# Converting w1 and w2 in the attention, and one operand's sum moved ahead of its split, in an attention and two-MoE kernel

## The chip, the cores and the metric

The kernel runs on one core of a Trainium2 chip. The core has a matrix engine (TensorE, PE in the profile; its weight loads are listed as PEld), a vector engine (VectorE, DVE), a scalar engine (ScalarE, ACT), a general engine (GpSimd, POOL) and a queue engine that here issues the transfers (SyncE, SP). Each takes its instructions in order and waits on semaphores for the others. The metric is the device time of one execution in microseconds (us); lower is better.

## The reference

Three stages follow one another. The inputs are float32, except the weights, which come as float64.

```python
# 1: attention with a local band and a few global columns, 4 x 8 heads of 768 x 64
scores = scale * q @ k.T + bias          # bias: -slope[h] * distance
a = softmax(where(keep, scores, -1e9))   # keep: column < 8, or 0 <= row - column < 96
x = a @ v                                # 3072 tokens x 512
# 2: first MoE layer, w_in 512 x 2048, w_out 2048 x 512
h = x @ w_in
x = (h * clip(h + 3, 0, 6) / 6) @ w_out
# 3: second MoE layer, w1 and w2 512 x 1024, w3 1024 x 1024, w_out 1024 x 512
out = ((x @ w1) * (x @ w2)) @ w3 @ w_out
```

## The kernel before

**Numbers.** Matmuls take a value as two parts, a high half rounded by ScalarE and a low half (the value less the high half), and a product is three matmuls: high by high, low by high, high by low. The low halves are made on VectorE or GpSimd. A weight comes as float64, 512 KB for 128 x 512 values. Its conversion to float32 is one ScalarE step (line 158, tile `cva`) and three VectorE steps on the raw bits (lines 171, 173 and 175, tile `cvt`).

**Weight jobs.** All weights go through one list of jobs, `wjobs`. A job is loaded by SyncE into a tile `st` (three buffers), converted, and handed to what it is for. `w_steps` does this in rounds of four ticks, and the code that writes the order calls `tick` in between: 4 ticks per step of the attention while the first weights are awaited, 2 after that, so one job for two steps; in the MoE stage a tick for every 0.5 or 1.2 us of TensorE's work. At a round a job waits for its load in ScalarE's queue (line 158), and in the next rounds its VectorE steps are written. A job whose source is float32 skips these four steps and gets to its use after as many rounds.

**The attention** runs 96 steps, two to a pair of score matmuls (line 419). A step's scores go through a maximum on VectorE (429), an exponential on ScalarE (438), a normalisation on GpSimd (446), a transpose and the product with v. A filler puts matmuls of the first MoE layer (half of its columns, `gen_a`) between. Sixteen pieces of w_in and w_out for the other half are converted here too and kept in DRAM (`wb`, line 591: a store from `cvt`).

**The rest of the first MoE layer** follows from 440 us on, in eight passes of 384 tokens, each `first` (gates: line 513 on ScalarE, 514 on VectorE, halves 497 and 500) and `second`, whose results are added up on VectorE (line 832, `part`), which frees the accumulators. Beside it, w3 times the last w_out is made (`gen_w34`), and w1 and w2 are prepared in sixteen quarters (`wt_job`): three VectorE sums (lines 687 to 689), then high halves on ScalarE (184) and low halves on GpSimd (185) of the quarter and of the sums. The quarters of the first two groups stay in place; the others go to DRAM and back.

**The second MoE layer** takes two token blocks at a time as a 2 x 2 problem with seven products in place of eight (`gen_ab`), for two groups of columns (`gg`), and then multiplies by the w3 and w_out product (`gen_out`). The seven token operands of the next pair are made meanwhile by `x_prep`: seven pieces, each a VectorE sum or nothing, then `put`, which makes the high half on ScalarE (783) and the low half on GpSimd (784). One piece is called after each of the products 6, 7, 5, 2, 4 and 3 of the second group, the seventh after the first two output blocks. Six of the eight pairs are followed by another one and so have pieces; before the first pair, `weave` puts the seven pieces between the last matmuls of `second`.

`s[0]` holds first a21 + a22, which is operand 5 and the start of `s[1]`, and then a12 - s[1], operand 3. The fourth piece was

```python
def s1():
    put(5, s[0])                                                  # ScalarE and GpSimd read s[0]
    nc.vector.tensor_tensor(s[0], a12, s[1], ALU.subtract)        # line 797 writes it
```

After each product VectorE adds it to the sums (line 901) and, for finished ones, multiplies both halves (896); the result is split into `g4` to `g7` for `gen_out`.

Of the kernel before, what the change touches and what calls it, by code (L numbers as in the profile page):

```python
# [8 lines left out]
F32 = mybir.dt.float32  # L9
# [8 lines left out]
P = 128  # L18
# [56 lines left out]
def kernel(ctx: ExitStack, tc: tile.TileContext, q, k, v, n_global, n_local,  # L75
# [12 lines left out]
    NF2 = DF2 // P  # L88
# [3 lines left out]
    FB = NF - FA  # L92
# [12 lines left out]
    dr = ctx.enter_context(tc.tile_pool(name="dr", bufs=1, space=DRAM))  # L105
# [5 lines left out]
    w34 = dr.tile([NF2, 2, P, DM], F32, name="w34")  # L111
    wt = dr.tile([NF2, 4, P, 512], F32, name="wt")
    part2 = dr.tile([NT, DM], F32, name="part2")
    wb = dr.tile([2 * FB, P, 512], F32, name="wb")

    WA = [wap.tile([P, 512], F32R, name=f"wa{i}") for i in range(4 * FA)]

# [11 lines left out]
    def queue(src, then, key=None):  # L129
        wjobs.append((src, then, key))  # L130
        queued.add(key)
# [51 lines left out]
    def w_split(t, hi, lo, key):  # L183
        nc.scalar.activation(hi, t, AF.Copy)  # L184
        (nc.vector if key[0] in first_weights else nc.gpsimd).tensor_tensor(lo, t, hi.bitcast(F32), ALU.subtract)  # L185
# [404 lines left out]
    def keep(n):  # L590
        return lambda t, st: nc.sync.dma_start(wb[n], t)

    for n, (w, part) in enumerate([(w_in, kchunk)] * FB + [(w_out, rows)] * FB):
        queue(part(w, FA + n % FB), keep(n), ("wb", n))

    slot = FA * 24 * TA / per

    def nticks(s):
        return 1 if s < 4 else 4 if awaited("wi", "wo") else 2

    for s in range(NS + 3):
# [24 lines left out]
        n = nticks(s)  # L626
# [44 lines left out]
        fill.run(GAPS[0] / 4)  # L671
        tick()

    NG = NF2 // 2

    def wt_index(g, w, c):
        return (2 * g + w) * 2 + c  # L680

    def wt_job(n):
        def then(t, st):
            bl = t.rearrange("p (a c) -> p a c", c=P)
            tt = st.bitcast(F32)[:, 512:]
            tl = tt.rearrange("p (a c) -> p a c", c=P)
            nc.vector.tensor_tensor(tl[:, 0:2], bl[:, 1:4:2], bl[:, 0:2], ALU.subtract)
            nc.vector.tensor_tensor(tl[:, 2], bl[:, 3], tl[:, 0], ALU.subtract)
            nc.vector.tensor_tensor(tl[:, 3], bl[:, 2], tl[:, 2], ALU.subtract)
            to = WA[4 * n:4 * n + 4] if n < 8 else WA[24:28]  # L690
            for i, x in enumerate((t, tt)):
                w_split(x, to[i], to[2 + i], ("wt", n))

            def store():
                for i in range(4):
                    nc.sync.dma_start(wt[n - 8, i], to[i].bitcast(F32))
            if n >= 8:
                wstore.append(store)
        return then
# [6 lines left out]

    def wt_jobs(gs):
        for g in gs:
            for w, x in enumerate((w1, w2)):
                for c in range(2):  # L710
                    n = wt_index(g, w, c)
                    src = x.rearrange("(s c p) f -> c p s f", s=2, p=P)[c][:, :, 2 * g * P:2 * (g + 1) * P]
                    queue(src, wt_job(n), ("wt", n))

    quarters = [(w, c) for w in range(2) for c in range(2)]

    def gen_w34():

        ng = DF2 // 512
        for f in range(NF2):  # L720
            queue(rows(w_o2, f), O2[f], ("o2", f))
        wt_jobs([2])
        for f in range(NF2):
            for g in range(ng):
                queue(rows(w3, f)[:, g * 512:(g + 1) * 512], lambda t, st: got.append(t))
        wt_jobs([3])

        def trans(f):
# [12 lines left out]
        for f in range(NF2):  # L741
# [10 lines left out]
            for z in range(2):  # L752
                nc.sync.dma_start(w34[f, z], o[z].bitcast(F32))
        wt_jobs(range(NG // 2))

    def step(gen, gap=None):
# [20 lines left out]
    def x_prep(k, tmp):  # L777

        a11, a12, a21, a22 = (RA[i][:, 2 * c:2 * c + 2] for i in range(2) for c in range(2))
        s = [tmp() for _ in range(3)]  # L780

        def put(n, x):
            nc.scalar.activation(X[n][:, 0:2], x, AF.Copy)  # L783
            nc.gpsimd.tensor_tensor(X[n][:, 2:4], x, X[n][:, 0:2].bitcast(F32), ALU.subtract)  # L784

        def first_():
            nc.vector.tensor_tensor(s[0], a21, a22, ALU.add)  # L787
            nc.vector.tensor_tensor(s[1], s[0], a11, ALU.subtract)
            put(1, a11)

        def s3():
            nc.vector.tensor_tensor(s[2], a11, a21, ALU.subtract)  # L792
            put(7, s[2])

        def s1():
            put(5, s[0])
            nc.vector.tensor_tensor(s[0], a12, s[1], ALU.subtract)  # L797

        return [first_, lambda: put(6, s[1]), s3, s1, lambda: put(2, a12), lambda: put(4, a22),
                lambda: put(3, s[0])]  # L800

    def weave(gen, pieces, start, gap):

# [8 lines left out]
    for t in reversed(range(NTA)):  # L812
# [22 lines left out]
        if t == 0:  # L835
            fill.drain(pump)
            pump_all()
            flush()
            half.close()
            xo = fast.enter_context(tc.tile_pool(name="xo", bufs=1, side="right", reuse_waits="tile"))  # L840
            for n in range(5):
                X[1 + n] = xo.tile([P, CC, NA], F32R, name=f"x{n}")
            X[6], X[7] = xT[0]

            def st_tmp():
                t = cvp.tile([P, 1024], U32, tag="st", name="stmp", bufs=3)
                return t.bitcast(F32)[:, :2 * NA].rearrange("p (a n) -> p a n", a=2)

            pieces = x_prep(NTA // 2 - 1, st_tmp)
            gen = weave(gen, pieces, 600.0, 1800.0)  # L850
# [139 lines left out]
    for n, (p, j) in enumerate(order):  # L990
        nxt = order[n + 1][1] if n + 1 < len(order) else j
        pieces = x_prep(nxt, z_tmp) if nxt != j else []
        for gen in (gen_ab(p, j, nxt, pieces), gen_out(p, j, pieces)):
            for cost in gen:
                pass
        while pieces:
            pieces.pop(0)()
# [221 lines left out]
```

## Time and profile before

| | |
|---|---|
| median of three runs | 1223.22 us (1220.52 to 1224.03) |
| the profiled execution | 1222.52 us, its span 1220.7 us |
| TensorE busy | 1156.7 us, 95% |
| VectorE, ScalarE, GpSimd busy | 56%, 44%, 35% |
| mean granted clock of TensorE | 0.979 |
| HBM read, written | 112.72 MB, 51.38 MB |

Times inside the trace count from the first instruction. A wait is put down to the instruction that ended it; "idle before" in brackets is the time in which an engine stood before an instruction. A busy TensorE is not TensorE at its peak, since matmuls overlap: what it loses is read from the distance of the starts.

### The profile page before, as it was taken

Reading aid. Unit: us, or ns where it says so; the run is one execution under the profiler, and the core shown is the slowest. Engines: PE = TensorE matmul, PEld = TensorE weight load, DVE = VectorE, ACT = ScalarE, POOL = GpSimd, SP = SyncE. Lnnn points to the kernel's source line nnn. Section 1 sums busy time; section 2 is a strip of 40 time slices with the busy share of each in tenths; the row PEclk is TensorE's granted clock in tenths of the full one; section 3 lists DMA queues with packets and bytes.
Section 4 is the critical chain, followed back from the end, with each engine's and each line's share of the span. In section 5 each row is a group of like instructions: output and inputs, shape, how many; then the busy total and the mean of one; then the engine's idle time right before and its main releaser. Section 6 shows DMA issues by size and latency. Waiting matters only on the chain. (4 is left out here: it accounts for less than half of the span.)

```text
span 1220.7 us, 19580 instructions
## 1 busy us (share of the span) xinstructions
PE 1156.7 (95%) x7040; PEld 1070.3 (88%) x7040; DVE 679.3 (56%) x1495; ACT 535.4 (44%) x1282; POOL 430.3 (35%) x370
## 2 busy tenths in 40 slices
PE   6699999999999999998999998889999999999996
PEld 4488998999999999998899998889899899898895
DVE  4887766544444424368544374855374463565653
ACT  4787767666666645344324143441323311221310
POOL 2133334242333422256302044682443410533510
PEclk9699999999999999999999999999999999999998
DMA  7675867534253023456553556506203156134022
GB/s 167 186 224 140 227 166 219 174 78 130 56 145 78 6 71 121 173 183 231 190 183 94 189 190 224 174 18 222 86 19 104 46 186 218 52 105 155 14 90 90
DMA packets 185578, 165.50 MB, mean 136 GB/s; under 512 B 110720, under 2 KB 150656, under 8 KB 185472
## 3 DMA queue, kind: packets, MB, share of 16 engines
q1 hardware_dynamic: 185184, 164.15, 43.8%
q8 instruction: 58, 0.95, 0.3%
q14 instruction: 48, 0.39, 0.1%
q10 hardware_dynamic: 288, 0.00, 0.0%
HBM read 112.72 MB, written 51.38 MB: 134 GB/s over the span
## 5 line engine op out<-in xcount | busy, mean ns | idle before, releaser
L66 PE MATMUL b<-x,wa 128*128 128x384 f32 x960 | 173.4, 340 | 0.7 <-DVE part L832 0.7
L66 PEld LDWEIGHTS b<-x,wa 128*128 128x128 f32 x960 | 169.7, 188 | 1.7 <-issue 1.0
L446 POOL TENSOR_TENSOR e<-e,su 128x512 f32<-128x512 f32 (+1 forms) x96 | 93.0, 969 | 206.9 <-DVE su L445 169.4
L901 DVE TENSOR_TENSOR u<-b,u 128x768 f32<-128x768 f32 x112 | 105.2, 951 | 99.8 <-PE b L66 86.8
L514 DVE SCALAR_TENSOR_TENSOR t<-t,h 128x384 f32<-128x384 f32 x128 | 70.6, 551 | 125.7 <-ACT t L513 125.5
L438 ACT ACTIVATE e<-e,mx 128x256 f32<-128x256 f32 (+1 forms) x192 | 93.0, 492 | 15.7 <-DVE mx L429 15.3
L513 ACT ACTIVATE t<-h,c 128x384 f32<-128x384 f32 x128 | 73.8, 576 | 45.8 <-PE h L66 45.3
L158 ACT ACTIVATE cva<-st 128x512 f32<-128x512 f32 x72 | 48.1, 667 | 68.9 <-DMA st<-in_moe_w_dram 45.0
L429 DVE CUSTOM_DVE_ANT_0 e<-s,base 128x256 f32<-128x256 f32 (+1 forms) x192 | 69.1, 397 | 2.3 <-PE s L419 1.8
L175 DVE SCALAR_TENSOR_TENSOR cvt<-cva,cvt 128x512 uint32<-128x512 uint32 x72 | 67.3, 935 | 1.4
L66 PE MATMUL h<-xt0h,wa 128*128 128x384 f32 x256 | 67.9, 341 | 0.0
L66 PE MATMUL h<-xt1h,wa 128*128 128x384 f32 x256 | 67.2, 339 | 0.0
L472 PE MATMUL pv<-p,rv 128*64 128x128 f32 x704 | 53.8, 291 | 13.9 <-ACT p L461 13.9
L454 PE MATMUL pt<-ident,e 128*128 128x128 f32 x352 | 59.1, 290 | 7.3 <-DVE kl L360 4.6
L461 ACT ACTIVATE p<-pt 128x512 f32<-128x512 f32 (+1 forms) x96 | 55.0, 573 | 24.8 <-PE pt L454 24.6
L472 PEld LDWEIGHTS pv<-p,rv 128*64 128x64 f32 x704 | 38.9, 141 | 28.2 <-ACT p L461 16.7
L500 POOL TENSOR_TENSOR g0l<-t,g0h 128x384 fp32r<-128x384 f32 x16 | 18.0, 1123 | 127.9 <-ACT g0h L497 127.9
L173 DVE SCALAR_TENSOR_TENSOR cvt<-st,cvt 128x512 uint32<-128x512 uint32 x72 | 62.2, 864 | 1.1
L896 DVE TENSOR_TENSOR u<-u 128x384 f32<-128x384 f32 x64 | 60.3, 943 | 1.6
L185 POOL TENSOR_TENSOR wa<-cvt,wa 128x512 fp32r<-128x512 f32 x24 | 34.5, 1440 | 64.5 <-ACT wa L184 56.0
L454 PEld LDWEIGHTS pt<-ident,e 128*128 128x128 f32 x352 | 42.8, 148 | 15.2 <-issue 12.3
L500 POOL TENSOR_TENSOR g3l<-u,g3h 128x384 fp32r<-128x384 f32 x8 | 8.1, 1018 | 135.1 <-ACT g3h L497 135.1
(435 smaller groups left out, 3121.4 us busy)
## 6 DMA issues: line engine op xcount, KB each, us to landing
st<-in_moe_w_dram SPq DMA_DIRECT2D x32, 512.0 KB, 5.5
st<-in_moe_w_out_dram SPq DMA_DIRECT2D x24, 512.0 KB, 4.2
st<-in_moe_w_in_dram SPq DMA_DIRECT2D x16, 512.0 KB, 4.4
wt<-wa SPq DMA_DIRECT2D x32, 256.0 KB, 3.8
wa<-wt SPq DMA_DIRECT2D x32, 256.0 KB, 5.3
rk<-in_k_dram SPq DMA_DIRECT2D x64, 96.0 KB, 3.8
rq<-in_q_dram SPq DMA_DIRECT2D x64, 96.0 KB, 3.0
rv<-in_v_dram SPq DMA_DIRECT2D x64, 96.0 KB, 2.9
```

The lines of the kernel that those rows point to most:

```text
L66: nc.tensor.matmul(out, a, b, start=(first and i == 0 and j == 0), stop=(last and i == n - 1 and j == 2))
L173: nc.vector.scalar_tensor_tensor(tu, low, 29, tu, ALU.logical_shift_right, ALU.bitwise_or)
L175: nc.vector.scalar_tensor_tensor(tu, au, 0x80000000, tu, ALU.bitwise_and, ALU.bitwise_or)
L429: nc.vector.tensor_tensor_reduce(e[:, j, :W], d["sc"][j][:, :W], bs, -slope[2 * hp + j], 3.0e38, ALU.add, ALU.min, mx[:, j:j + 1])
L438: nc.scalar.activation(e[:, j, :W], e[:, j, :W], AF.Exp, bias=mx[:, j:j + 1], scale=-1.0, accum_out=su[:, j:j + 1])
L446: nc.gpsimd.tensor_tensor(d["e"][:, :, :W], d["e"][:, :, :W], su.unsqueeze(2).to_broadcast([P, 2, W]), ALU.mult)
L454: nc.tensor.transpose(ps[:, t, j, :], d["e"][:, j, t * P:(t + 1) * P], ident)
L472: nc.tensor.matmul(ps[D * j:D * j + D, half], raw[i][2][:, c0 + t, j, :], d["p"][:, t, j, :], start=(t == 0), stop=(t == nk - 1))
L513: nc.scalar.activation(t, h, AF.Relu, bias=c3)
L514: nc.vector.scalar_tensor_tensor(t, t, 6.0, h, ALU.min, ALU.mult)
L896: nc.vector.tensor_tensor(x[:, 0], x[:, 0], x[:, 1], ALU.mult)
L901: nc.vector.tensor_tensor(o, x[:, :, :NA], y, ALU.add)
```

## The change

Two edits. First, sixteen more jobs are queued behind the sixteen pieces that are converted in the attention: w1 and w2, in the same quarters, converted and kept in DRAM. The jobs in the MoE stage load these float32 pieces. Second, the subtraction for operand 3 moves from the fourth piece of `x_prep` to the seventh, ahead of its own `put`.

```diff
-    wb = dr.tile([2 * FB, P, 512], F32, name="wb")
+    wb = dr.tile([2 * FB + 2 * NF2, P, 512], F32, name="wb")
...
+    for n in range(2 * NF2):
+        g, w, c = n // 4, (w1, w2)[n // 2 % 2], n % 2
+        queue(w.rearrange("(s c p) f -> c p s f", s=2, p=P)[c][:, :, 2 * g * P:2 * (g + 1) * P], keep(2 * FB + n),
+              ("wb", 2 * FB + n))
...
     def wt_jobs(gs):
         for g in gs:
-            for w, x in enumerate((w1, w2)):
-                for c in range(2):
-                    n = wt_index(g, w, c)
-                    src = x.rearrange("(s c p) f -> c p s f", s=2, p=P)[c][:, :, 2 * g * P:2 * (g + 1) * P]
-                    queue(src, wt_job(n), ("wt", n))
+            for w, c in quarters:
+                n = wt_index(g, w, c)
+                queue(wb[2 * FB + n], wt_job(n), ("wt", n))
...
-        def s1():
-            put(5, s[0])
+        def s4():
             nc.vector.tensor_tensor(s[0], a12, s[1], ALU.subtract)
-
-        return [first_, lambda: put(6, s[1]), s3, s1, lambda: put(2, a12), lambda: put(4, a22),
-                lambda: put(3, s[0])]
+            put(3, s[0])
+
+        return [first_, lambda: put(6, s[1]), s3, lambda: put(5, s[0]), lambda: put(2, a12), lambda: put(4, a22), s4]
```

Line numbers shift: 687 to 689 become 691 to 693, 797 becomes 798, 832 becomes 833, 896 and 901 become 897 and 902.

VectorE around the start of a pass of `first`, where the first w1 quarter of the last eight is prepared, before:

```order
L171 TENSOR_SCALAR cvt<-cva 128x512
L173 SCALAR_TENSOR_TENSOR cvt<-st,cvt 128x512
L832 SCALAR_TENSOR_TENSOR part<-x_8694,part 128x384
L175 SCALAR_TENSOR_TENSOR cvt<-cva,cvt 128x512
L514 SCALAR_TENSOR_TENSOR t<-t,h 128x384
L687 TENSOR_TENSOR st<-cvt 128x256
```

and in the changed kernel:

```order
L833 SCALAR_TENSOR_TENSOR part<-x_8790,part 128x384
L514 SCALAR_TENSOR_TENSOR t<-t,h 128x384
L691 TENSOR_TENSOR st<-st 128x256
```

The three conversion steps are gone from both sides of `part`; the first sum of the quarter stands behind the same gate as before, and now reads the loaded tile.

VectorE at the end of `second` for the last tokens, where the pieces are woven in, before:

```order
L792 TENSOR_TENSOR stmp<-xt1h,xt1l 128x768
L797 TENSOR_TENSOR stmp<-xt1h,stmp 128x768
L832 SCALAR_TENSOR_TENSOR part<-x_9263,part 128x384
L832 SCALAR_TENSOR_TENSOR part<-x_9264,part 128x384
L832 SCALAR_TENSOR_TENSOR part<-x_9335,part 128x384
```

and in the changed kernel:

```order
L794 TENSOR_TENSOR stmp<-xt1h,xt1l 128x768
L833 SCALAR_TENSOR_TENSOR part<-x_9311,part 128x384
L833 SCALAR_TENSOR_TENSOR part<-x_9312,part 128x384
L798 TENSOR_TENSOR stmp<-xt1h,stmp 128x768
L833 SCALAR_TENSOR_TENSOR part<-x_9382,part 128x384
```

The subtraction moved behind two of the four additions.

VectorE in the second group of `gen_ab`, from the third piece to the split of `g6`, before:

```order
L792 TENSOR_TENSOR stmp<-xt1h,xt1l 128x768
L901 TENSOR_TENSOR u<-b,u 128x768
L896 TENSOR_TENSOR u<-u 128x384
L797 TENSOR_TENSOR stmp<-xt1h,stmp 128x768
L901 TENSOR_TENSOR u<-b,u 128x768
L896 TENSOR_TENSOR u<-u 128x384
L500 TENSOR_TENSOR g5l<-u,g5h 128x384
L901 TENSOR_TENSOR u<-b,u 128x768
L896 TENSOR_TENSOR u<-u 128x384
L500 TENSOR_TENSOR g6l<-u,g6h 128x384
```

and in the changed kernel:

```order
L794 TENSOR_TENSOR stmp<-xt1h,xt1l 128x768
L902 TENSOR_TENSOR u<-b,u 128x768
L897 TENSOR_TENSOR u<-u 128x384
L902 TENSOR_TENSOR u<-b,u 128x768
L897 TENSOR_TENSOR u<-u 128x384
L500 TENSOR_TENSOR g5l<-u,g5h 128x384
L902 TENSOR_TENSOR u<-b,u 128x768
L897 TENSOR_TENSOR u<-u 128x384
L500 TENSOR_TENSOR g6l<-u,g6h 128x384
L798 TENSOR_TENSOR stmp<-xt1h,stmp 128x768
```

The subtraction moved from ahead of the addition of product 4 to behind the last split.

## Rows read from the trace of the kernel before

**Rows 1.** Busy by stretch: PE, PEld, DVE, ACT, POOL; granted clock, DMA share, GB/s.
```profile
250.00:300.00 50.00, 49.78 (x385) 46.21 (x383) 23.51 (x101) 32.62 (x98) 17.61 (x18) 1.00 0.43 113
...
750.00:800.00 50.00, 43.95 (x225) 42.37 (x226) 42.98 (x63) 23.77 (x44) 31.57 (x25) 0.93 0.52 170
```
**Rows 2.** Timeline of PE at one pair's output blocks: start, us, instruction [idle before].
```profile
960.82 0.40 PE L66 MATMUL b<-wob1h,g2l 128*128 128x512 f32 x1
961.06 0.39 PE L66 MATMUL b<-wob1l,g2h 128*128 128x512 f32 x1
962.32 0.50 PE L66 MATMUL b<-wob2h,g5h 128*128 128x512 f32 x1 [0.87 <-ACT g5h L497]
962.91 0.50 PE L66 MATMUL b<-wob2h,g5l 128*128 128x512 f32 x1
```
**Rows 3.** Waits of the whole span: us in total, times, longest.
```profile
PE b L66 <- ACT g5h L497: 5.2, 6, 0.9
```
**Rows 4.** Timeline of DVE, same pair.
```profile
959.29 0.96 DVE L797 TENSOR_TENSOR stmp<-xt1h,stmp 128x768 f32<-128x768 f32 x1 [4.52 <-POOL x L784]
960.17 0.95 DVE L901 TENSOR_TENSOR u<-b,u 128x768 f32<-128x768 f32 x1
```
**Rows 5.** Groups of instructions by form: busy us, mean ns, idle before.
```profile
L797 DVE TENSOR_TENSOR stmp<-xt1h,stmp 128x768 f32<-128x768 f32 x7 | 8.3, 1186 | 32.5 <-POOL x L784 32.5
```
**Rows 6.** Timeline of POOL, same pair.
```profile
957.42 1.84 POOL L784 TENSOR_TENSOR x<-stmp,x 128x768 fp32r<-128x768 f32 x1
```
**Rows 7.** Timeline of DVE in the woven pieces.
```profile
820.60 2.55 DVE L797 TENSOR_TENSOR stmp<-xt1h,stmp 128x768 f32<-128x768 f32 x1 [5.36 <-POOL x L784]
```
**Rows 8.** Waits of PE from 440 to 870 us.
```profile
PE h L66 <- DVE part L832: 4.2, 1, 4.2
PE h L66 <- DVE t L514: 4.0, 3, 2.5
PE x L66 <- DVE part L832: 2.7, 1, 2.7
PE x L66 <- POOL g7l L500: 2.7, 2, 1.8
PE x L66 <- POOL g5l L500: 2.6, 2, 1.3
PE x L66 <- POOL g6l L500: 1.2, 2, 0.6
```
**Rows 9.** Timeline of ACT at the wait of 4.2 us.
```profile
749.87 0.66 ACT L158 ACTIVATE cva<-st 128x512 f32<-128x512 f32 x1 [8.54 <-DMA st<-in_moe_w_dram]
```
**Rows 10.** Timeline of DVE, same place.
```profile
751.70 0.55 DVE L832 SCALAR_TENSOR_TENSOR part<-x,part 128x384 f32<-128x384 f32 x1
```
**Rows 11.** Timeline of SyncE's queue, same place.
```profile
743.88 1.16 SPq L149 DMA_DIRECT2D st<-in_moe_w_dram  x2
```
**Rows 12.** Busy and clock of a stretch with a slow piece.
```profile
740.00:760.00 20.00, 15.77 (x81) 15.46 (x80) 8.59 (x14) 6.76 (x13) 7.50 (x7) 0.91 0.71 222
```
**Rows 13.** Timeline of PE: the scores that begin three stretches of twelve pairs.
```profile
120.92 0.39 PE L419 MATMUL s<-kh,qh 64*128 64x256 f32 x2
...
230.37 0.39 PE L419 MATMUL s<-kh,qh 64*128 64x256 f32 x2
...
337.99 0.39 PE L419 MATMUL s<-kh,qh 64*128 64x256 f32 x2
```
**Rows 14.** Groups of instructions by form, 120 to 231 us.
```profile
L446 POOL TENSOR_TENSOR e<-e,su 128x512 f32<-128x512 f32 x21 | 21.8, 1040 | 39.3 <-DVE su L445 37.3 <-ACT cva L158 2.0
...
L175 DVE SCALAR_TENSOR_TENSOR cvt<-cva,cvt 128x512 uint32<-128x512 uint32 x12 | 13.1, 1093 | 0.0
...
L173 DVE SCALAR_TENSOR_TENSOR cvt<-st,cvt 128x512 uint32<-128x512 uint32 x12 | 9.5, 791 | 0.1
L158 ACT ACTIVATE cva<-st 128x512 f32<-128x512 f32 x12 | 8.0, 668 | 0.0
```
**Rows 15.** The same, 231 to 338 us.
```profile
L446 POOL TENSOR_TENSOR e<-e,su 128x512 f32<-128x512 f32 x20 | 20.8, 1040 | 35.1 <-DVE su L445 25.3 <-PE pt L454 7.8 <-PE x L66 1.1
```

## The prediction

> **What bounds the kernel now.** I read the busy time by stretch first. In the stretch of the attention TensorE is busy 49.8 of 50 us at full clock while VectorE has half its time free; at 750 to 800 us TensorE falls to 44.0 and its clock to 0.93, and VectorE is at 43.0 [rows 1]. So the end is set by TensorE in order, and what can be won are its idle spots. I then listed its waits. They are of two kinds.
>
> The first stands in the last third, where seven products of a token pair and then the output blocks run. Each output block is 512 columns and starts 0.24 us after the one before; ahead of the third factor block the start comes 1.26 us later and the next again 0.59 us later [rows 2]. The wait is for `g5h`, six times in all [rows 3]. `g5` comes from the addition of product 4 on VectorE, and that addition started at 960.17 because the subtraction of line 797 ahead of it sat idle 4.52 us [rows 4]. All seven such subtractions together waited 32.5 us [rows 5], and the one at 959.29 started when a GpSimd subtraction that began at 957.42 and took 1.84 us was over [rows 6]: it reads `s[0]`, the tile which line 797 writes again. That is a wait for a tile that is still read, not for data.
>
> The same subtraction waited 5.36 us at 815 to 820 us and then ran 2.55 us [rows 7]; queued behind it stood the four additions `part` that free TensorE's accumulators.
>
> The second kind are the waits of 440 to 870 us [rows 8]: one of 4.2 us and one of 2.7 us for `part`, 4.0 us for the gate on VectorE, and 6.5 us (2.7, 2.6, 1.2) for the low halves `g5l` to `g7l` from GpSimd. All but the 2.7 lie where w1, w2 or w3 are converted. The 4.2 us is a chain I followed back: ScalarE's first conversion step stood 8.54 us for the load of a w1 piece [rows 9], the VectorE steps queued behind it, and `part` behind these ran at 751.70 only [rows 10]; the load had been issued at 743.88 [rows 11]. After such a gap the mean granted clock of 20 us is 0.91, that is, some of it at 1.2 GHz, or 1.8 us of TensorE's time lost [rows 12]; there are four such stretches from 580 to 840 us, 1.8 us each.
>
> **The change part by part.** *The last operand's sum.* Line 797 goes behind the additions of products 4 and 3, so no addition stands behind it any more; it comes when the first two output blocks are done. It removes from each of six cycles (1.26 - 0.24) + (0.59 - 0.24) = 1.37 us [rows 2], together 8.2 us. What is late next: the addition of product 4 may start when VectorE has ended the work before, at 954.8 (959.29 less the 4.52 of waiting, [rows 4]), five microseconds earlier, while its result is needed at 961.3 (961.06 + 0.24, [rows 2]); so nothing is late there. In the new place it delays the additions of later output blocks by some 1.0 us each time, and no matmul waits for these soon; ScalarE's and GpSimd's split of the operand follows it as before, and the operand is needed only at the seventh product of the next pair: the rest of the output blocks and 72 matmuls of the six products before it come first. The transfers that reload its sources wait for this reading; they had to wait for the last split of another operand from the same tile before. Bounds: 0 (a new wait takes its place) to 9.
>
> In the woven pieces at 808 to 835 us the subtraction now stands behind two of the four additions. The 2.7 us wait for `part` goes, and with it the slow stretch behind it, 1.8 us: 4.5 us. What stays late is the third addition, behind the subtraction; the accumulator it frees is not wanted before the next stage. Bounds 0 to 4.5.
>
> *The conversion moved out of the MoE stages.* Sixteen pieces lose one ScalarE step and three VectorE steps each, and their loads fall from 512 to 256 KB. In the chain of the 4.2 us wait no conversion stands ahead of `part`, so the wait and its slow stretch go: 6.0 us. What is late next is the first sum of the quarter (line 687, now 691), which waits for the load in VectorE's queue behind the first gate; from the old landing, 6 us after issue for two 512 KB pieces, I estimate 4 us for half the bytes, so that the gate behind it comes an estimated 0.8 us too late for an accumulator. I take 5.2, bounds 0 to 6.0.
>
> The 6.5 us for low halves: ScalarE and VectorE have less to do in each round, but GpSimd still makes two low halves for each piece, and ScalarE still waits in order for the three sums of the quarter. I take half of it, 3.2 us. In the first of the two places (570 us) I give what is won back to the 2.5 us wait at 593, which hangs on a load of w3 that stays as large as it is, except 1.0 us; so 1.6 + 1.0, and the slow stretch at 760 to 780 us, 1.8: 4.4. Bounds 0 to 12.6 (6.5 + 2.5 + two slow stretches). Of the two shorter gate waits (4.0 - 2.5 = 1.5) I take 1.0; one stands right behind the last conversion.
>
> *The conversion added in the attention.* The kernel before shows it: the same steps for the pieces of w_in and w_out run from 127 to 229 us, twelve of them between the pairs of scores that start at 120.92 and 230.37, and the next twelve pairs from there to 337.99 have none [rows 13]. 109.45 against 107.62 us: 1.83 us for twelve, so 2.4 us for sixteen. The new ones run in the same loop, one for two steps, until some 375 us. The loads and stores join SyncE's queue between the unit loads, as those twelve did, so the price has them in it. The twelve cost VectorE 13.1 + 9.5 us in two of the three steps and ScalarE 8.0 us [rows 14]: nearly all of it lies beside matmuls. If that cover were gone, the sixteen would cost 16/12 x 30.6 = 40.8 us. Bounds 0 to 40.8; I take the nearest row, 2.4.
>
> The GpSimd normalisation of the softmax took 1040 ns with the conversions beside it and 1040 ns without [rows 14, 15]; the conversion steps themselves took 791 and 1093 ns. The Trainium skill speaks against the move here: "SBUF — State Buffer", section "Who interferes with whom", says that a VectorE instruction with two inputs from SBUF and a GpSimd instruction that reads SBUF block one another, whoever comes second waiting. By that rule both long steps, which have two such inputs, could hold the normalisation; the trace shows the other order, the conversions grow and the normalisation does not, so the sum stays.
>
> *Sum.* 8.2 + 4.5 + 5.2 + 4.4 + 1.0 = 23.3 us won, 2.4 lost, 20.9 net. The profiled execution took 1222.5 us (span 1220.7), so 1201.6; the median of the runs is 0.7 us above it, so 1202.
>
> **The rivals.** *A, the stalls at the weight pieces stay.* GpSimd's two low halves and ScalarE's in-order wait bound the rounds, and the first sum waits for its load as the conversion did. For it: the waits name GpSimd, whose work does not shrink; against it: GpSimd is busy 31.6 of 50 us there [rows 1], and VectorE, which is fuller, is relieved. Then 8.2 + 4.5 - 2.4 = 10.3: 1212.
>
> *B, the moved subtraction wins nothing.* It stands before additions that wait for the reload of partial outputs, and the operand or the reload of its sources comes too late for the next pair, so the stall moves. Against it speak the 72 matmuls that come before its use. Then 5.2 + 4.4 + 1.0 - 2.4 = 8.2: 1215.
>
> *C, slower.* In the attention at 240 to 375 us VectorE's queue holds the score maxima behind the conversion, and ScalarE's the exponentials; if the whole of both lands on the way to the transposes, 40.8 us are lost against 23.3 won: 1241. It decides from 1.5 us a piece on (23.3/16); the twelve before cost 0.15 each, and that is what speaks against it.
>
> *D, everything goes.* All the waits named and their slow stretches vanish: 8.2 + 4.5 + 6.0 + 12.6 + 1.5 = 32.8, attention free: 1190.
>
> **How the numbers follow.** The forecast 0.60, with its own range 1195 to 1209 (half of the 4.4 and of the 5.2 either way, and the 8.2 by two); A 0.18, B 0.07, C 0.05, D 0.10. A range of 1192 to 1214 holds the forecast, A and the nearer edges of B and D, about 0.83. A change under 0.3% (3.7 us) can't be told from none in a measurement of this kernel: faster 0.93, within 0.03, slower 0.04.
>
> **What would show it.** In the changed profile the six waits for `g5h` are gone and the subtraction waits for nothing; the wait of 2.7 us for `part` at 820 is gone; the one of 4.2 us at 748 is under 1; the clock stretches at 740 to 780 and 820 to 840 us read 1.00; twelve pairs in the middle of the attention take 109.5 instead of 107.6 us. Wrong would be: a wait of the first sum on its load that holds `part` or the gate, low halves as late as now, or attention pairs longer by more than 1 us each.

## The result, and the profile after

| | before | after |
|---|---|---|
| median of four runs | 1221.93 us (1220.52 to 1224.03) | 1203.86 us (1202.58 to 1205.29) |
| the profiled execution | 1222.52 us, span 1220.7 | 1203.56 us, span 1201.8 |
| TensorE busy | 1156.7 us | 1144.0 us |
| mean granted clock of TensorE | 0.979 | 0.983 |

The ratio is 0.9851, 95% interval 0.983 to 0.9872: faster by 18 us, where 21 were forecast. The two traces can be cut at three instructions that both have: the last score matmul of the attention, the first matmul of the seven products, and the last matmul of all.

| stretch | before | after | moved | forecast |
|---|---|---|---|---|
| start to the last score | 428.3 | 430.5 | +2.2 | +2.4 |
| to the first matmul of the products | 402.1 | 387.1 | -15.0 | -15.1 (4.5 + 5.2 + 4.4 + 1.0) |
| products and output blocks | 380.0 | 371.1 | -9.0 | -8.2 |
| last matmul to the span's end | 10.3 | 13.1 | +2.8 | none |

Three stretches came out as forecast within a microsecond, the second in part because misses inside it cancel, as the account of the prediction below shows. The fourth I had not looked at.

**The products.** The matmuls of the output blocks (the timeline of PE, columns as in [rows 2]) now follow one another without a break at the third factor block:

```profile
945.29 0.39 PE L66 MATMUL b<-wob1l,g2h 128*128 128x512 f32 x1
945.52 0.39 PE L66 MATMUL b<-wob2h,g5h 128*128 128x512 f32 x1
945.75 0.40 PE L66 MATMUL b<-wob2h,g5l 128*128 128x512 f32 x1
```

The starts are 0.23 us apart, where they stood 1.26 and 0.59 us in [rows 2]; no wait for `g5h` is left in the list of [rows 3]. The timeline of DVE in the same pair shows why:

```profile
938.92 0.95 DVE L902 TENSOR_TENSOR u<-b,u 128x768 f32<-128x768 f32 x1
...
942.36 0.94 DVE L902 TENSOR_TENSOR u<-b,u 128x768 f32<-128x768 f32 x1
943.34 1.23 DVE L897 TENSOR_TENSOR u<-u 128x384 f32<-128x384 f32 x1
...
946.62 2.59 DVE L798 TENSOR_TENSOR stmp<-xt1h,stmp 128x768 f32<-128x768 f32 x1
```

The addition of product 4 starts at 938.92, 6.6 us ahead of the matmul at 945.52 that needs its result; in [rows 4] it was 2.2 us ahead (960.17 against 962.32). The subtraction stands last and with no idle time before it. All seven of them, as a group by form, idled 2.6 us in place of the 32.5 of [rows 5]:

```profile
L798 DVE TENSOR_TENSOR stmp<-xt1h,stmp 128x768 f32<-128x768 f32 x7 | 13.2, 1887 | 2.6 <-POOL x L786 2.6
```

**The woven pieces and the waits from 440 to 870 us.** The list of PE's waits, to be read beside [rows 8]:

```profile
PE wt L738 <- DVE cvt L175: 2.5, 2, 2.0
PE h L66 <- DVE t L514: 2.4, 2, 1.6
PE x L66 <- POOL g5l L500: 2.0, 2, 1.3
PE b L66 <- DVE part L833: 0.7, 1, 0.7
PE x L66 <- DVE part L833: 0.7, 1, 0.7
PE x L66 <- POOL g6l L500: 0.4, 2, 0.2
PE x L66 <- POOL g7l L500: 0.3, 1, 0.3
```

Before, `part` cost 7.6 us: the 6.9 of [rows 8] and 0.7 right ahead of the products (at 830.44 us), which [rows 8] does not show; 1.4 are left, that 0.7 among them. Of 6.5 for low halves 2.7 are left. The first row was not in [rows 8]: it is a wait for w3, where what was won at 570 us was given back, as the prediction said of that place. PE's timeline has it at 585 us, and behind it the late gate:

```profile
582.10 0.44 PE L66 MATMUL x<-g0h,wob0h 128*128 128x384 f32 x1 [0.68 <-DVE part L833]
585.07 0.63 PE L738 MATMUL wt<-ident,cvt 128*128 128x128 f32 x4 [2.00 <-DVE cvt L175]
597.66 0.44 PE L66 MATMUL h<-xt0h,wib3h 128*128 128x384 f32 x1 [1.63 <-DVE t L514]
```

**The place of the 4.2 us wait.** SyncE's queue and then DVE, which answer to [rows 11] and [rows 10]:

```profile
743.17 0.96 SPq L149 DMA_DIRECT2D st<-wb  x2
```
```profile
744.91 0.56 DVE L833 SCALAR_TENSOR_TENSOR part<-x,part 128x384 f32<-128x384 f32 x1 [2.49 <-DMA part<-p]
747.16 0.56 DVE L514 SCALAR_TENSOR_TENSOR t<-t,h 128x384 f32<-128x384 f32 x1 [1.69 <-ACT t L513]
748.34 0.42 DVE L691 TENSOR_TENSOR st<-st 128x256 f32<-128x256 f32 x1 [0.61 <-DMA st<-wb]
...
752.06 0.55 DVE L514 SCALAR_TENSOR_TENSOR t<-t,h 128x384 f32<-128x384 f32 x1 [1.65 <-ACT t L513]
```

`part` runs at 744.91, with no conversion ahead of it, and the first sum stands 0.61 us for its load, which took 5.2 us from issue to the end of that wait (748.34 less 743.17). The gate that stands behind the first sum in VectorE's queue, at 752.06, is ready at 752.61, and the matmul that needs the accumulator it frees starts without a wait:

```profile
752.67 0.44 PE L66 MATMUL h<-xt1h,wib4h 128*128 128x384 f32 x1
```

The clock, by stretches as in [rows 12]:

```profile
740.00:760.00 20.00, 19.29 (x109) 18.78 (x107) 7.78 (x13) 6.75 (x13) 10.06 (x10) 1.00 0.48 164
760.00:780.00 20.00, 18.47 (x93) 17.71 (x94) 8.95 (x18) 7.15 (x14) 14.00 (x12) 0.91 0.57 183
...
820.00:840.00 20.00, 20.00 (x116) 20.00 (x115) 13.38 (x14) 4.34 (x7) 5.91 (x5) 1.00 0.78 278
```

Of the four slow stretches of the kernel before, three read 1.00 now (the one from 580 to 600 us as well, where the waits are not shorter); the one from 760 to 780 us stays at 0.91 behind the waits for low halves that are left. Which stretch is slow also differs between executions: sum_only below, with the same wait of 4.2 us, reads 0.83 from 740 to 760 us where the kernel before reads 0.91.

**The attention.** The scores that begin the stretches of twelve pairs, beside [rows 13]:

```profile
120.53 0.39 PE L419 MATMUL s<-kh,qh 64*128 64x256 f32 x2
...
229.96 0.39 PE L419 MATMUL s<-kh,qh 64*128 64x256 f32 x2
...
339.39 0.39 PE L419 MATMUL s<-kh,qh 64*128 64x256 f32 x2
...
429.78 0.39 PE L419 MATMUL s<-kh,qh 64*128 64x256 f32 x2
```

109.43 and 109.43 us: the second stretch, now with twelve conversions of its own, costs what the first does (107.62 before, with one). The ten pairs from there to the last take 90.39 us with five conversions, against 89.60 before. So the sixteen cost 1.81 + 0.79 = 2.6 us. The +2.2 of the table is this less 0.4 us by which the first stretch begins earlier here, and that is chance: the scores at 120.53 begin between 119.5 and 122.4 us in the twelve traces whose kernels do not differ ahead of them (all but w3_early), while the stretches behind them repeat to within 0.04 us where the conversions are the same.

**The end.** The last instruction that both chains of waits have ahead of the kernel's final branch is `flagi` on VectorE. After:

```profile
core 0 of [0], span 1201.8 us
...
1191.73 0.14 DVE flagi L344
```

and before:

```profile
core 0 of [0], span 1220.7 us
...
1213.71 0.14 DVE flagi L344
```

From its end to the span's end it is 9.9 us after and 6.9 us before (1220.7 - 1213.85). In between SyncE passes the branch over the general path and closes the kernel. In the records of the kernel after, two of SyncE's closing semaphore waits stand 2.8 us apart (1197.57 and 1200.36), with no other engine to wait for, and packets of 8 KB of the instruction queue fall between them (1197.62 and 1197.87). They alone show little: they belong to a burst of five, and the kernel before has such a burst beside its closing waits too (1218.87 to 1219.44), without a stand. No transfer of the kernel is awaited either: the last one has landed at 1193.20. The pages say which engine's program grew; after

```profile
span 1201.8 us, 19626 instructions
...
PE 1144.0 (95%) x7040; PEld 1063.7 (89%) x7040; DVE 684.6 (57%) x1495; ACT 535.5 (45%) x1282; POOL 433.9 (36%) x370
```

and before

```profile
span 1220.7 us, 19580 instructions
...
PE 1156.7 (95%) x7040; PEld 1070.3 (88%) x7040; DVE 679.3 (56%) x1495; ACT 535.4 (44%) x1282; POOL 430.3 (35%) x370
```

The counts of the four computing engines are equal; the sixteen conversions only changed their place. The 46 instructions more are not among them: SyncE has 55 records more (1189 against 1134) for the loads and stores of the pieces, the other engines together nine fewer.

### The profile page after: what moved, and what is told of

The parts are those of the page before. It is cut to its first block, busy times and chain, and to the rows that moved or that the text cites. A ratio compares the mean times of both kernels' runs of the same rounds, so it can differ in the third digit from the quotient of the medians.

```text
span 1201.8 us, 19626 instructions
## 1 busy us (share of the span) xinstructions
PE 1144.0 (95%) x7040; PEld 1063.7 (89%) x7040; DVE 684.6 (57%) x1495; ACT 535.5 (45%) x1282; POOL 433.9 (36%) x370
## 4 chain that ended last, share of the span: by engine, by line
PE 81%; DVE 6%; DMA 4%; ACT 3%; SPq 2%; issue 2%; POOL 1%; POOLq 0%; DVEq 0%; ACTq 0%
PE b L66 30%; PE x L66 19%; PE h L66 17%; PE wo L66 3%; PE pv L472 3%; PE s L419 3%; PE pt L454 3%; SPq L259 1%; DMA st<-in_moe_w_dram 1%; PE pk L372 1%; POOL wa L185 1%; DVE e L429 1%; DVE kl L360 1%; DVE cvt L175 1%; DVE cvt L173 1%
## 5 line engine op out<-in xcount | busy, mean ns | idle before, releaser
L454 PE MATMUL pt<-ident,e 128*128 128x128 f32 x352 | 58.7, 288 | 10.6 <-DVE kl L360 7.4
L185 POOL TENSOR_TENSOR wa<-st,wa 128x512 fp32r<-128x512 f32 x32 | 43.2, 1358 | 46.0 <-ACT wa L184 31.7
L173 DVE SCALAR_TENSOR_TENSOR cvt<-st,cvt 128x512 uint32<-128x512 uint32 x72 | 57.7, 801 | 0.9
```

The costliest lines, as they stand in the source:

```text
L173: nc.vector.scalar_tensor_tensor(tu, low, 29, tu, ALU.logical_shift_right, ALU.bitwise_or)
L454: nc.tensor.transpose(ps[:, t, j, :], d["e"][:, j, t * P:(t + 1) * P], ident)
```

## The experiments

The experiments ran in three groups (the first four, the next four and the last three), each with the kernel before beside it, whose medians were 1223.35, 1223.53 and 1220.47 us. Each ratio is to the kernel before of its group, and kernels of different groups are compared by ratio.

**sum_only**: the subtraction moved alone.

```diff
-        def s1():
-            put(5, s[0])
+        def s4():
             nc.vector.tensor_tensor(s[0], a12, s[1], ALU.subtract)
+            put(3, s[0])
```

> The kernel before with the moved subtraction alone. Theory: the six waits for g5h go and each pair with pieces takes 46.35 us instead of 47.85 (9.0 us), and the 2.7 us wait for part near 820 us with the slow clock stretch behind it goes (4.5 us): 13.5 us less, 1208.5 us against 1222. Rival: the 820 us wait goes only where the weights' conversions are out of the way too, then 9.0 us: 1213. Rival B of the prediction (the stall only moves): 1222.

1210.83 us, 0.9889 (0.9861 to 0.9918). PE's waits from 440 to 870 us:

```profile
PE h L66 <- DVE part L831: 4.2, 1, 4.2
...
PE b L66 <- DVE part L831: 0.7, 1, 0.7
```

The wait of 2.7 us is gone, the one of 4.2 has stayed, and all pairs take 46.35 us. So both waits that the prediction put down to this edit are its own; B falls. From the last score to the products 397.6 us against 402.1: 4.5 us, the size forecast.

**weights_only**: the other edit alone.

```diff
+    for n in range(2 * NF2):
+        g, w, c = n // 4, (w1, w2)[n // 2 % 2], n % 2
+        queue(w.rearrange(...)[c][:, :, 2 * g * P:2 * (g + 1) * P], keep(2 * FB + n), ("wb", 2 * FB + n))
...
-                    queue(src, wt_job(n), ("wt", n))
+                queue(wb[2 * FB + n], wt_job(n), ("wt", n))
```

> The changed kernel with the subtraction back in the fourth piece. Theory: attention 2.2 us longer, the first MoE layer's passes 7.7 us shorter around 745 to 790 us, 1 to 2 us at each of 560 to 600 and 802 us: 8 us less than before, 1213.5 us. Rival A of the prediction (the stalls at the weight pieces stay): 1223 or above. If the two parts help one another, this and the subtraction alone together fall short of the whole change's 18 us by more than 3.

1217.15 us, 0.9952 (0.9934 to 0.9969). In the waits of the whole span the six for `g5h` are as in [rows 3]:

```profile
PE b L66 <- ACT g5h L497: 5.6, 6, 1.2
```

The gain, 6.2 us, is some 2 us short of what I expected, and the end has the stand: from `flagi` to the span's end 10.0 us. The two edits add up within the intervals: 0.9889 x 0.9952 = 0.984, and together they gave 0.9851.

**attn_only**: the conversion in the attention is added, the later jobs still load and convert float64. Its result is not used.

```diff
+    for n in range(2 * NF2):
+        g, w, c = n // 4, (w1, w2)[n // 2 % 2], n % 2
+        queue(w.rearrange(...)[c][:, :, 2 * g * P:2 * (g + 1) * P], keep(2 * FB + n), ("wb", 2 * FB + n))
```

> The kernel before with the sixteen conversions and stores added in the attention, whose results nobody reads: the MoE stage converts w1 and w2 as before. Theory: only the price, 2.2 to 2.5 us in the attention: 1224.5 us, each group of six pairs about 0.9 us longer. Rival C: the price is larger than twelve earlier pieces showed because ScalarE's and VectorE's steps delay the softmax: 1230 or above. Rival: hidden, 1222.

1228.66 us, 1.004 (1.0026 to 1.0054): 5.3 us lost, twice what the attention costs. In its profiled execution the last score comes at 430.83 (+2.5), and the end takes 9.7 us in place of 6.9 (+2.9). (That execution, 1225.05 us, is one of the two fastest of the ten. It also wins 3.2 us between the attention and the products, so its span is only 2.4 us longer; of these, 2.3 are waits for the gate on VectorE, 1.7 us there against the 4.0 of [rows 8].) The added work has two prices, and only one of them lies where it is added.

**late_only**: the later jobs load float32 pieces without a conversion, nothing is added in the attention.

```diff
-                    queue(src, wt_job(n), ("wt", n))
+                queue(wb[n], wt_job(n), ("wt", n))
```

> The kernel before, in which the MoE stage takes sixteen float32 pieces that are in DRAM anyway (those of w_in and w_out) in place of w1 and w2, so nothing is converted for them at all and nothing is added in the attention; the products use wrong weights. Theory: the gain of the late half without the price: 10 to 11 us less, 1211.5 us, and 2 to 3 us below the kernel with the weights moved alone. Rival: without the price, but also without gain, because low halves and loads bound these rounds: 1221.

1212.9 us, 0.9912 (0.9881 to 0.9944): 10.5 us won, the end as before (6.8 us). The trace has the same 10.5 us between the last score and the products (391.6 against 402.1). So the gain of the conversions' leaving is 10.5, which the forecast had at 10.6 (5.2 + 4.4 + 1.0), and the 6.2 of weights_only are, within the noise, this less the two prices (10.5 - 2.6 - 2.8 = 5.1).

**bytes_same**: the later jobs load 512 KB of float32, so the conversion is gone and the bytes are not.

```diff
+            t = t[:, :512]
...
-                queue(wb[2 * FB + n], wt_job(n), ("wt", n))
+                m = 2 * FB + min(n, 2 * NF2 - 2)
+                queue(wb[m:m + 2].rearrange("n p f -> p n f"), wt_job(n), ("wt", n))
```

> The changed kernel whose late loads of w1 and w2 bring 512 KB of float32 (a piece and the one behind it, of which half is used; the last of the sixteen quarters gets the weights of the one before it), so that the bytes are those of before and only the conversions are gone. Theory: the wait of 4.2 us near 748 stays gone, because part no longer stands behind the load, and the first sum waits some 2 us longer for its load: 1 to 2 us more than the changed kernel. Rival: the smaller load was what helped: 6 us more or above, with the wait near 748 back.

1206.22 us, 0.9864 (0.9843 to 0.9885), beside after_again at 1204.93: 1.3 us. The `part` of 748 us is still early; it is the sum and the gate behind it that come later, as DVE's timeline shows:

```profile
747.76 0.56 DVE L835 SCALAR_TENSOR_TENSOR part<-x,part 128x384 f32<-128x384 f32 x1 [2.52 <-DMA part<-p]
...
752.64 0.43 DVE L692 TENSOR_TENSOR st<-st 128x256 f32<-128x256 f32 x1 [2.06 <-DMA st<-wb]
```

The sum waits 2.06 us in place of 0.61. So the conversions' place in VectorE's order, not the size of the load, made the 4.2 us wait; the size is worth little. Through the gate behind that sum it costs TensorE a wait of 1.31 us (at 756.97), which the kernel after does not have; the 1.3 us of the runs lie within their intervals.

**after_again**: the kernel after, unchanged, beside the next three.

> The changed kernel once more, beside the three next to it on the same chip. 0.983 to 0.987 of before; in its trace SyncE stands some 2.8 us between the last two semaphore waits of the program, as it did in the three kernels with the added conversions and in none of the three without.

1204.93 us, 0.9851 (0.9826 to 0.9875). The stand is there again: the two closing waits of SyncE are 2.7 us apart.

**pad12**: twelve transfers of 8 bytes in SyncE's stream, at one place.

```diff
+        if n == 4:
+            for i in range(12):
+                nc.sync.dma_start(pad[i:i + 1], nbits[0:1, 0:2])
```

> The changed kernel with twelve transfers of 8 bytes more in SyncE's queue in the second MoE layer, read by nobody: the code behind them moves by at least twelve instructions. Theory: the 2.8 us at the end is SyncE fetching the next block of its code, whose border fell between the last waits since the sixteen loads and stores were added; moved, it falls elsewhere: 2.8 us less than the changed kernel. Rival: the wait is for a transfer or a semaphore that the added work itself delays: no change, 0 us.

1204.2 us, 0.9846 (0.9825 to 0.9868): no change, and the end still takes 9.7 us. This left the explanation open: either the stream's length doesn't matter, or twelve are too few. w3_early spoke for the second: its stream is longer by 67 records than that of the kernel after, and its end took 6.9 us.

**w3_early**: all of w3 converted in the attention as well, at three ticks a step instead of two so that it gets done there.

```diff
+    for n in range(2 * NF2):
+        queue(rows(w3, n // 2)[:, n % 2 * 512:(n % 2 + 1) * 512], keep(2 * FB + 2 * NF2 + n),
+              ("wb", 2 * FB + 2 * NF2 + n))
...
-        return 1 if s < 4 else 4 if awaited("wi", "wo") else 2
+        return 1 if s < 4 else 4 if awaited("wi", "wo") else 3 if awaited("wb") else 2
...
-                queue(rows(w3, f)[:, g * 512:(g + 1) * 512], lambda t, st: got.append(t))
+                queue(wb[2 * FB + 2 * NF2 + f * ng + g], lambda t, st: got.append(t))
```

> The changed kernel with w3 converted in the attention too, in three ticks a step in place of two. Theory: sixteen more pieces cost 2.4 us, and the waits left at 580 to 600 us, for w3's conversion (2.5 us) and the gate behind it (1.6 us), go: 2 us less than the changed kernel, 2.8 more if the border of the code moves as well. Rival: attention at three pieces in four steps has DMA at 0.85 of its time or more and unit loads come late: slower than the changed kernel by 3 us or more.

1216.07 us, 0.9941 (0.9918 to 0.9963), 11 us above after_again. The last score comes at 452.2 in place of 430.5: 21.7 us lost in the attention, against 5.5 won up to the products and 2.9 at the end. The waits of all engines from 120 to 340 us:

```profile
DVE cvt L171 <- DMA wb<-cvt: 7.8, 4, 2.4
...
ACT cva L158 <- DMA st<-in_moe_w_dram: 6.7, 5, 2.5
...
PE s L419 <- DVE mx L429: 6.1, 4, 1.8
```

The two stretches of twelve pairs that begin at 121.44 and 239.57 take 118.13 and 116.75 us, with eighteen conversions each, where the kernel after takes 109.43 with twelve. None of the three waits is in that list of the kernel after. The first conversion step now waits in VectorE's queue for a `cvt` whose store is not out, the score maxima stand behind it, and the scores wait for these; ScalarE waits for loads with the exponentials behind. That is rival C: its mechanism is real, and the pace decides it. Busy time and clock by stretch say the same, here

```profile
231.00:340.00 109.00, 103.15 (x783) 95.42 (x784) 76.42 (x243) 73.62 (x213) 38.60 (x39) 0.97 0.76 218
```

and in the kernel after

```profile
231.00:340.00 109.00, 106.53 (x842) 98.89 (x843) 72.84 (x244) 75.26 (x220) 40.18 (x40) 1.00 0.68 188
```

842 matmuls in 109 us fell to 783, and the granted clock with them.

**pad60**: sixty transfers of 8 bytes, ten ahead of each of the pairs two to seven.

```diff
+        if 1 <= n <= 6:
+            for i in range(10):
+                nc.sync.dma_start(pad[n - 1, i:i + 1], nbits[0:1, 0:2])
```

> The kernel after with sixty transfers of 8 bytes added to SyncE's stream, ten ahead of each of the pairs two to seven, where SyncE has idle time; nothing reads them. Theory (the stand of 2.8 us at the end is a fetch of SyncE's own instructions, and whether it comes depends on how long the stream is): the stream grows from 1189 to about 1259 records, near the 1256 of the kernel with w3 converted early, in which the stand was gone, so it should be gone here too: from the last matmul to the span's end 10.2 us in place of 13.1, and the time about 2.5 us below that of the kernel after, 1201. Rival (the stand belongs to what the attention does, or to TensorE's or the vector engine's stream): it stays, 13.1 us, and the time is that of the kernel after, 1204.

1201.79 us, 0.9844 (0.9823 to 0.9866). The chain of waits ends:

```profile
core 0 of [0], span 1199.1 us
...
1191.17 0.14 DVE flagi L344
```

7.8 us in place of 9.9, and the stand of 2.8 us is not in SyncE's records; the 0.9 us that are left over 6.9 lie ahead of the closing waits. The ratio alone can't be told from that of the kernel after (0.9851).

**w3_tail**: of w3 only the first five pieces, behind w1 and w2 at their pace.

```diff
+    for n in range(5):
+        queue(rows(w3, n // 2)[:, n % 2 * 512:(n % 2 + 1) * 512], keep(2 * FB + 2 * NF2 + n),
+              ("wb", 2 * FB + 2 * NF2 + n))
...
+                n = f * ng + g
+                src = wb[2 * FB + 2 * NF2 + n] if n < 5 else rows(w3, f)[:, g * 512:(g + 1) * 512]
```

> The kernel after with the first five pieces of w3 converted in the attention too, behind w1 and w2 and at the same pace of one piece for two steps. Theory (the pace, not the number of pieces, is what made the attention dear when all of w3 was converted at three ticks a step): the six pairs from 375 to 430 us are still free of conversions, and five pieces cost 5 x 0.15 = 0.8 us there; of the waits of TensorE between 580 and 600 us, 5.4 us in the kernel after, three to four go. Net -2 to -3, about 1202. Rival (each piece beyond the sixteen costs what those of the run at three ticks cost, 21.7/16 = 1.4 us): 6.8 lost against 4 won, 1207. A third: the waits only move on to the sixth piece and the time is that of the kernel after.

1197.29 us, 0.9808 (0.9786 to 0.983). The last score comes at 430.36, no later than in the kernel after, but only because the first stretch of twelve pairs begins 1.0 us earlier here (119.51). The last ten pairs, where the five conversions stand, take 91.27 us in place of 90.39:

```profile
338.39 0.39 PE L419 MATMUL s<-kh,qh 64*128 64x256 f32 x2
...
429.66 0.39 PE L419 MATMUL s<-kh,qh 64*128 64x256 f32 x2
```

So the five cost 0.9 us, where 0.8 were expected. PE's waits from 440 to 870 us begin with:

```profile
PE x L66 <- POOL g5l L500: 2.0, 2, 1.3
PE x L66 <- POOL g7l L500: 1.0, 2, 0.5
PE h L66 <- DVE t L514: 0.8, 1, 0.8
```

The wait for w3 is gone altogether, the late gate at 597 with it. I expected three to four us of waits to go; the trace gives 6.0 from the last score to the products (381.1 against 387.1). Of these, 4.1 are waits: all 4.8 us between 580 and 600 us are gone, since the sixth piece is not late either (the expectation had 5.4 there), and the low half `g7l` is awaited 0.7 us longer. The other 1.8 are the stretch from 760 to 780 us, which reads 1.00 here; that w3 brings this about is not shown. For w3_early it says that five pieces beyond the sixteen are cheap at one for two steps, 0.18 us each, so the pace, not the number, is the likely cause there.

**w3_tail_pad**: both, with eight transfers a pair.

> Both at once: five pieces of w3 early, and eight transfers of 8 bytes ahead of each of the pairs two to seven, which bring SyncE's stream to about 1265 records. If both theories hold, the wins add: -2 to -3 for w3 and -2.5 for the end, about 1199, below both kernels. If the stand at the end has nothing to do with the stream's length, this is as the run with w3 alone; if w3 costs more than it wins, it is above the run with the padding alone.

1196.36 us (1195.85 to 1197.29), 0.9799 (0.9777 to 0.9821), the fastest of all, beside 1197.29 (1196.95 to 1198.53) of w3_tail. Its chain ends:

```profile
core 0 of [0], span 1194.6 us
...
1187.53 0.14 DVE flagi L344
```

6.9 us, as in the kernel before; w3_tail without the padding has 9.7. The runs gain 0.9 and not 2.8, and their ranges overlap: in the profiled executions the padded kernel is already 2.1 us late at the last score, before any padding comes, and 2.0 of these at the first stretch of twelve pairs (121.55 against 119.51), within the spread of that point. Whether the timed runs have that too their times don't show.

## Why the prediction was right, and where it was not

*The last operand's sum* was right in its mechanism, its two places and nearly in its size. 8.2 us were mis-sized: it was 9.0, 1.5 a pair. I had added two late starts of [rows 2]; the third matmul behind them also started 0.34 us after its forerunner in place of 0.24, and that tenth is the difference.

*The subtraction's cost in its new place* was off: 1.0 us was forecast, it takes 2.59. No matmul waits for it (all pairs take 46.35 us each), so it did not enter the sum.

*The woven pieces*, 4.5: sum_only alone gives 4.5.

*The conversions' leaving* came out right in its sum, 10.5 in late_only against 10.6, and this is in part luck. In the two traces, with 1.8 us for each slow stretch as in [rows 12], the places are:

| place | forecast | in the traces |
|---|---|---|
| 560 to 600 us | 1.0 | 2.2: 0.4 of waits, 1.8 of the stretch from 580 to 600 us |
| 740 to 800 us | 8.6 (5.2 + 1.6 + 1.8) | 7.5: 5.7 of waits, 1.8 of the stretch from 740 to 760 us |
| 803 us | 1.0 (for two short waits for the gate) | 0.9 |

The misses are these. The 5.2 were 6.0 less a gate 0.8 us late behind the first sum; that gate is not late (752.67 above), and the 0.8 in the list of waits belong to a later one, where the kernel before waited 0.6. The load was estimated at 4 us from issue to landing, and 5.2 were measured up to the end of the wait. The slow stretch of 760 to 780 us, counted as gone, stayed, and the one of 580 to 600 us, not counted as gone, went. The low halves fell from 6.5 to 2.7, a little more than the half that I took. And what was won at 570 us (2.6 of waits) was given back to w3 behind it (2.2), as forecast; w3_tail showed that it is to be had.

*The attention*, 2.4: 2.6 in the stretches that hold the conversions, 2.2 in the table. The row was the right one, with one reading wrong: the twelve pairs said to have no conversion have one, at 233.93 us, so 1.83 us are the price of eleven, and sixteen come to 2.7. That the price would not hold at any pace w3_early showed.

*What the prediction did not contain* is the end: it took for granted, without a term for it, that the span ends as long after the last matmul as before. It costs 2.8 us, is there in after, after_again, weights_only, attn_only, pad12, bytes_same and w3_tail, and not in before, sum_only, late_only, w3_early and w3_tail_pad; in pad60 most of it is gone. Shown is that the added conversions bring it and that SyncE's stream alone can take it away: attn_only has it with the late jobs unchanged, sixty or forty-eight idle transfers remove it, twelve do not, each in one trace. By records of SyncE it is there at 1189, 1203 and 1205, and not at 1134, 1253, 1256 and 1257. It is no wait for a transfer: in pad12 and w3_tail the last transfer signals another semaphore, and the stand is between the same two waits. That it is a fetch of SyncE's instructions is inferred from the packets of the instruction queue: each of the seven traces with the stand has a further one of 8 KB 0.6 us behind it (0.75 to 0.77 us ahead of the span's end), and none of the six others has one there. Against a plain border in the code that moves with the stream's length, as pad12 assumed, speaks that the stand keeps its place at 1189, 1203 and 1205 records. Which instructions the fetch brings, and at which lengths it comes, stays open.

Of the rivals, A fell with the 4.2 us wait and the low halves, B with sum_only, D with the waits that are left. C's mechanism is what w3_early ran into.

## What to carry to other kernels

An instruction that overwrites a tile still being read holds all that stands behind it on its engine: look for an idle spot whose releaser is a reader, and move the writer behind the last instruction that another engine awaits. Work moved under a stage that has room is cheap at the pace at which the trace has shown it to be cheap; five pieces more at that pace cost 0.9 us and saved 4.1 of waits, one and a half times the pace cost 22 us. A small price is read from stretches that repeat, not from the time since the start, which varied by 2.9 us here at 120 us. Check the time from the last matmul to the span's end when a queue engine's program gets longer.

## What the runs showed of the hardware

The moved subtraction took 0.96 us where it waited for GpSimd [rows 4] and takes 2.59 us where it runs beside it; the product of halves on VectorE takes 1.23 us there and 0.57 alone. GpSimd pays too. Its splits at that time, in the timeline of POOL:

```profile
944.11 2.17 POOL L786 TENSOR_TENSOR x<-xt1h,x 128x768 fp32r<-128x768 f32 x1
...
950.17 1.84 POOL L786 TENSOR_TENSOR x<-stmp,x 128x768 fp32r<-128x768 f32 x1 [1.77 <-ACT x L785]
```

2.17 us beside VectorE, 1.84 without it, as in [rows 6]. The Trainium skill, "SBUF — State Buffer", section "Who interferes with whom", says that a VectorE instruction with two inputs from SBUF contends with a GpSimd instruction that reads SBUF; here the trace agrees, with 2.59 against 0.96 and 2.17 against 1.84. For the normalisation of the attention it agrees as well, on one side. The third conversion step starts while a normalisation runs, and it is the step that grows, by what they overlap: 1.11 us with 0.56 us of overlap, 1.38 with 0.83. The normalisation, the first of the two each time, keeps its 1040 ns, with twelve conversions beside it in the second stretch as in [rows 15] with one.

The stand at the end was new to me: 2.8 us that came with the conversions and went with idle transfers added to one engine's instruction stream.
